# Two matrix products without a reader, placed among the first units of a retention-plus-MLP kernel

## The chip, the cores and the metric

The kernel runs on one core of one Trainium2 chip. Its time is device time in microseconds (us) of one launch on that core. TensorE is called PE in the profile, VectorE DVE, ScalarE ACT, GpSimd POOL and SyncE SP.

## What is computed

The reference has two stages. The first is a recurrent retention layer with 4 batches, 8 heads, 768 positions and head size 64:

```python
gamma = 1.0 - 2.0 ** (-5.0 - np.arange(H, dtype=np.float32))
scale = 1.0 / np.sqrt(D)
for t in range(S):
    state = gamma[None, :, None, None] * state + np.einsum('bhd,bhe->bhde', k[:, :, t], v[:, :, t])
    y[:, :, t] = scale * np.einsum('bhd,bhde->bhe', q[:, :, t], state)
```

Its output is laid out as x with 3072 rows (batch and position) and 512 columns (head and feature). The second stage is `h = x @ w_in; g = h * sigmoid(h); out = g @ w_out`, with w_in 512 x 2048 and w_out 2048 x 512.

## The kernel before

**Units and chunks.** The 768 positions are cut into 6 chunks of 128. A pair (chunk, batch) is a *unit*; there are 24, numbered chunk by chunk, so that units 0 to 3 are chunk 0 of the four batches. For each unit PE does three things, in functions that a hand-written order calls by short names:

- `T(n)` (`stage_t`, line 442): eight transposes of 128x128 through `ident` (L456), four of k and four of q, into two PSUM banks; ACT copies them out (L457).
- `SC(n)` (lines 767 to 771): the sums k^T v (`stage_s`, L482) and the scores (`stage_a`, L492), 16 small products each, into the tile `sc`. Each works on a 64x64 quarter of PE's array, and each is two records in the trace. `A(n)` then runs the next step of `steps_a`: DVE multiplies the scores by the decay mask into `am` (L500), ACT or DVE makes `mid` (L506 or L508), DVE the new `state` (L512). `Q(n)` scales the transposed q (L412), `K(n)` scales k (L407).
- `YA(n)` and `YB(n)` (`stage_y`, L531): the unit's outputs, 16 products with `am` and then those with `mid` and, after chunk 0, with `state`; between the two halves of the latter PE waits for a one-element POOL instruction (`fence`, L386). `X(n)` steps through `steps_y` and `split_x`: ACT copies the output out of PSUM (L572), and ACT and DVE split it into three fp32r parts `xt` (L587, L590, L593).

**The first product.** `P(n)` (`multiply`, line 680) is one block of x @ w_in for a whole chunk: 8 products of 512 columns into `ha` and 4 into `hb` (L684). `P(0)` needs the `xt` parts of units 0 to 3 and the first block of w_in, which ACT and DVE convert from 64-bit to 32-bit words and split (`W(i)`, lines 192 to 251 and 114 to 128). Then ACT copies `ha` (L694), DVE subtracts `hb` (L699) and ACT applies SiLU (L704).

**PSUM.** `turn(name)` (line 377) hands out the banks h0, h1 and h2 in rotation; the k half of `T(n)`, `ha` and `hb` take one each. `banks("q")`, `banks("s")` and `banks("y")` are fixed places for the q half of `T`, for `sc` and for `y`.

**Order.** Up to line 916 the order on all five engines is the order in which the program writes the calls (lines 802 to 915). PE keeps the written order to the end. After line 916 a planner orders the other engines, and the loop over `steps` (lines 961 to 1000) does the remaining first products with the remaining units folded between them. The last part (lines 1003 to 1054) is the second product, `o`, `oa` and `ob` (L1025), with g read back from DRAM.

**Around the change** (lines 823 to 834), `T`, `YA`, `YB` and `SC` are the calls that put work on PE:

```python
    X(1)
    T(3), K(3)
    X(1), X(1)
    YA(2), YB(2), X(2)
    SC(3), A(3), A(3), Q(3), A(3)
    X(2), W(1), W(1)
    X(2), X(2)
    YA(3), YB(3), X(3), X(3)
    W(1), W(1)
    T(4)
```

On PE this is: transposes of unit 3, outputs of unit 2, scores of unit 3, outputs of unit 3, transposes of unit 4, and then `P(0)`.

Of the kernel before, what the change touches and what calls it, by code (L numbers as in the profile page):

```python
# [33 lines left out]
def kernel(  # L34
# [28 lines left out]
    nc = tc.nc  # L63
    B, H, S, D = q.shape
    DM, DF = moe_w_in.shape
    C = 128
# [250 lines left out]
    ident = const.tile([128, 128], FP32, tag="ident", name="ident")  # L317
# [54 lines left out]
    def banks(tag, name, n=2):  # L372
        return ps_u.tile([128, n, 512], FP32, tag=tag, name=name)

    turns = [0]

    def turn(name):
        turns[0] += 1
        return ps_h.tile([128, 512], FP32, tag=f"h{turns[0] % 3}", name=name)
# [62 lines left out]
    def stage_t(n):  # L442
# [23 lines left out]
        for o in range(2):  # L466
            for i in range(2):
                evac[:] = [nc.scalar.copy(out=made[i][:, :, ts(o, D)], in_=tp[o][:, i]).ins]

    def score_tile(n):  # L470
        u = banks("s", f"sc_{n}")
        sc, sums = (u[:, :, ts(i, 4 * D)].rearrange("p o (a t) -> p o a t", a=HP)
                    for i in range(2))
        return sc, sums

    def stage_s(n, sums):

        kf, vs = kqv["k"].pop(n), kqv["v"][n]
        for a in range(HP):
            for o in range(2 if units[n][0] < NC - 1 else 1):  # L480
                for j in range(2):
                    nc.tensor.matmul(sums[ts(j, D), o, a, :], lhsT=kf[ts(o, D), 2 * a + j, :],  # L482
                                     rhs=vs[ts(o, D), 2 * a + j, :], start=True, stop=True,
                                     skip_group_check=True)

    def stage_a(n, sc):

        ktn = kt.pop(n)
        for a in range(HP):
            for o in range(2):  # L490
                for j in range(2):
                    nc.tensor.matmul(sc[ts(o, D), j, a, :], lhsT=ktn[ts(j, D), a, ts(o, D)],  # L492
                                     rhs=qt[n][ts(j, D), a, ts(o, D)], start=True, stop=True,
                                     skip_group_check=True)

    def steps_a(n, sc, sums):

        c, b = units[n]
        am[n] = one.tile([128, 2, HP, D], FP32, tag="am", name=f"am_{n}")
        mask = nc.vector.tensor_tensor(out=am[n], in0=sc, in1=decay, op=ALU.mult).ins  # L500
        masked[:] = [mask]
        yield
        mid = one.tile([128, HP, D], FP32, tag="mid", name=f"mid_{n}", bufs=2)
        steps_of[n] = state.get(b), mid
        if c == 0:
            nc.scalar.copy(out=mid, in_=sums[:, 0])  # L506
        else:
            nc.vector.tensor_tensor(out=mid, in0=state[b], in1=sums[:, 0], op=ALU.add)  # L508
        yield
        if c < NC - 1:  # L510
            state[b] = one.tile([128, HP, D], FP32, tag="state", name=f"state_{n}", bufs=B + 2)
            nc.vector.tensor_tensor(out=state[b], in0=mid, in1=sums[:, 1], op=ALU.add)  # L512
# [8 lines left out]
    def stage_y(n):  # L521

        vs, amn, qtn = kqv["v"].pop(n), am.pop(n), qt.pop(n)
        states = steps_of.pop(n)
        yp = banks("y", f"y_{n}")[:, :, : 4 * D].rearrange("p o (a t) -> p o a t", a=HP)

        started, done, new = set(), [], []

        def product(a, o, j, lhsT, rhs):
            e = j ^ (a % 2)  # L530
            i = nc.tensor.matmul(yp[ts(e, D), o, a, :], lhsT=lhsT, rhs=rhs,  # L531
                                 start=(e, o) not in started, stop=True,
                                 skip_group_check=True).ins
            started.add((e, o))
            if new:
                fence(done[-1], i)
                new.clear()
            done.append(i)

        def scores():  # L540
            for a in range(HP):
                for o in range(2):
                    for j in range(2):
                        product(a, o, j, vs[ts(o, D), 2 * a + j, :], amn[ts(o, D), j, a, :])

        def states_with(part):

            new.extend([part] * part)
            for a in range(HP):
                for o in range(2):  # L550
                    j = o ^ part
                    if states[o] is not None:
                        product(a, o, j, states[o][ts(j, D), a, :], qtn[ts(j, D), a, ts(o, D)])

        return scores, states_with, yp
# [6 lines left out]
    def steps_y(n, yp):  # L562
        c, b = units[n]
        if b == 0:
            p, tag = (wpool, "wq") if c == LATE else (xpool, "xt")
            xt[c] = p.tile([128, 3, KIN, NT], FP32R, tag=tag, name=f"xt_{c}")
        raw = None
        if c < LATE:
            if n == 0:
                raws.append(wpool.tile([128, LATE * B, KIN, C], FP32, tag="wq", name="ys"))  # L570
            raw = raws[0][:, n]
            nc.scalar.copy(out=raw.rearrange("p a (o t) -> p o a t", o=2), in_=yp)  # L572
        elif c == LATE:
            raw = hpool.tile([128, KIN, C], FP32, tag="hs", name=f"ys_{n}")
            nc.scalar.copy(out=raw.rearrange("p a (o t) -> p o a t", o=2), in_=yp)
            nc.sync.dma_start(out=y_dram[b], in_=raw)
        yield from split_x(c, b, yp, raw)
# [50 lines left out]
    def halves(m):  # L628
# [9 lines left out]
        if mid:  # L638
            sc, sums = score_tile(m - 1)
            stage_s(m - 1, sums)  # L640
            stage_a(m - 1, sc)
            if 1 < m <= 3 * B + 1 and units[m - 1][1] == 0:
                next_chunk()

            with queue(taken_out[0]) if m > 3 * B + 1 else ExitStack():
                finish_a(m - 1, sc, sums)
            scale_q(m - 1)
            if m > 3 * B + 1 and units[m - 1][1] == B - 1:

                behind_copy.append(next_chunk)  # L650
# [113 lines left out]
    def T(n):  # L764
        stage_t(n)

    def SC(n):
        sa[n] = sc, sums = score_tile(n)
        stage_s(n, sums)
        stage_a(n, sc)  # L770
        asteps[n] = steps_a(n, sc, sums)

    def A(n):
        next(asteps[n], None)

    def YA(n):
        ys[n] = stage_y(n)
        ys[n][0]()
        ys[n][1](0)

    def YB(n):
        ys[n][1](1)
        ysteps[n] = steps_y(n, ys[n][2])

    def X(n):
        next(ysteps[n], None)
# [3 lines left out]
    def W(i, times=1):  # L790
        if i not in slices:
            slices[i] = early_slice(i)
        for _ in range(times):
            next(slices[i], None)
# [5 lines left out]
    K, Q = scale_k, scale_q  # L800
# [22 lines left out]
    X(1)  # L823
    T(3), K(3)
    X(1), X(1)
    YA(2), YB(2), X(2)
    SC(3), A(3), A(3), Q(3), A(3)
    X(2), W(1), W(1)
    X(2), X(2)
    YA(3), YB(3), X(3), X(3)  # L830
# [172 lines left out]
    for c in range(NC):  # L1003
# [9 lines left out]
        for f in range(NF):  # L1013
            n = c * NF + f
# [3 lines left out]
            t = ready[n]  # L1018
            if f >= early_f:
                continue  # L1020
            for b in range(B):
                gh, glo, gm = (t[:, i, ts(b, C)] for i in range(3))
                oa, ob = acc[b]
                for o, g, i in (oa, gh, 0), (oa, glo, 1), (ob, gm, 2):
                    nc.tensor.matmul(o, lhsT=g, rhs=wo[f][:, i, :], start=f == 0 and i != 1,  # L1025
                                     stop=f == NF - 1 and i != 0)

        for b in range(B if early_f < NF else 0):
            oa, ob = acc[b]
            for o, parts in (ob, (2,)), (oa, (0, 1)):  # L1030
                for f in range(early_f, NF):
                    for i in parts:
                        nc.tensor.matmul(o, lhsT=ready[c * NF + f][:, i, ts(b, C)],  # L1033
                                         rhs=wo[f][:, i, :], start=False,
                                         stop=f == NF - 1 and i != 0)
        for b in range(B):
# [11 lines left out]
            n = 2 if b == B - 1 else 1  # L1048
# [36 lines left out]
```

## Time and profile before

| What | us |
|---|---|
| median of 3 runs | 619.29 |
| lowest and highest of them | 618.85, 619.48 |
| the profiled execution's own time | 621.07 |
| its span, first to last instruction | 619.2 |
| PE busy in it | 602.0 |
| DVE busy | 424.0 |
| ACT busy | 315.2 |
| DMA, mean rate | 176 GB/s |

The profile lists, for every group of instructions, its line, engine, operation and tile, its start, its length and what ended the idle time before it. Matmul ends are modelled and overlap, so the pace of PE is read from starts rather than from lengths. "PEclk" is the share of its full clock that PE was granted; the trace keeps it as a list of stretches, each with one share. "Issue" names idle time in which the engine waited for no semaphore that the profile shows.

### The profile page before, as it was taken

The page shows a single profiled execution, that of the slowest core. Times are in us where ns is not written, and L with a number is a line of the kernel's source. Part 1 is how long each engine was busy: PE and PEld are TensorE (multiplying, and loading weights), DVE is VectorE, ACT ScalarE, POOL GpSimd, SP SyncE. Part 2 cuts the span into 40 slices and gives each one's busy share as a digit, 9 for nine tenths or more (in the row PEclk, how much of TensorE's full clock was granted, in tenths as well). Part 3 has the DMA queues.
Part 4 walks back from the last instruction along what each step waited for, and adds up shares of the span by engine and source line. Part 5 has one row for each costly group of instructions (what it writes and reads, how often), then busy time and mean ns, then how long its engine had stood idle before and what let it go on. Part 6 is the DMA issues. An engine that isn't in the chain of part 4 may idle for free.

```text
span 619.2 us, 13515 instructions
## 1 busy us (share of the span) xinstructions
PE 602.0 (97%) x5384; PEld 494.0 (80%) x5384; DVE 424.0 (68%) x731; ACT 315.2 (51%) x601; POOL 29.4 (5%) x85
## 2 busy tenths in 40 slices
PE   5899999999999999999999999999999999999997
PEld 4787787888778888888788888888888888888886
DVE  4789899889988877786699783645635453654631
ACT  7568897667667656655588742312221221412311
POOL 3000000100031111120000000000000000000000
PEclk9799999999999999999999999999999999999999
DMA  9997874685699599989977542532524333442301
GB/s 191 224 227 183 224 223 154 197 242 179 218 235 231 182 252 246 291 228 270 304 228 261 190 150 68 166 106 90 184 68 131 141 103 102 139 133 89 116 1 68
DMA packets 144334, 108.88 MB, mean 176 GB/s; under 512 B 101136, under 2 KB 109584, under 8 KB 144272
## 3 DMA queue, kind: packets, MB, share of 16 engines
q1 hardware_dynamic: 141392, 102.79, 59.4%
q10 hardware_dynamic: 2880, 5.24, 2.3%
q8 instruction: 42, 0.69, 0.5%
q14 instruction: 20, 0.16, 0.1%
HBM read 66.06 MB, written 36.70 MB: 166 GB/s over the span
## 4 chain that ended last, share of the span: by engine, by line
PE 73%; DVE 5%; DMA 2%; issue 2%; ACT 2%; DVEq 0%; POOLq 0%; ACTq 0%
PE o L1025 21%; PE ha L684 18%; PE oa L1025 14%; PE hb L684 9%; PE ob L1025 7%; PE y L531 2%; DMA gd<-g 2%; DVE g L699 1%; DVE ca L219 1%; PE sc L492 1%; PE sc L482 1%; DMA wf<-in_moe_w_in_dram 0%; DVE ca L216 0%; DVE cs L224 0%; PE o L1033 0%
## 5 line engine op out<-in xcount | busy, mean ns | idle before, releaser
L684 PE MATMUL ha<-xt,wi 128*128 128x512 f32 x768 | 195.4, 396 | 1.4 <-DVE g L699 0.6
L684 PEld LDWEIGHTS ha<-xt,wi 128*128 128x128 f32 x768 | 142.9, 189 | 34.2 <-ACT wi L126 1.4
L1025 PE MATMUL o<-wo,gs 128*128 128x512 f32 x564 | 143.2, 389 | 0.0
L751 DVE TENSOR_TENSOR gs<-gr,gs 128x512 fp32r<-128x512 f32 x96 | 62.2, 686 | 90.3 <-ACT gs L749 90.3
L1025 PEld LDWEIGHTS o<-wo,gs 128*128 128x128 f32 x564 | 105.9, 188 | 21.9
L749 ACT ACTIVATE gs<-gr 128x512 fp32r<-128x512 f32 x96 | 53.6, 621 | 134.2 <-issue 131.9
L1025 PE MATMUL oa<-wo,gs 128*128 128x512 f32 x376 | 115.8, 389 | 0.0
L684 PE MATMUL hb<-xt,wi 128*128 128x512 f32 x384 | 103.0, 390 | 0.2
L699 DVE TENSOR_TENSOR g<-g,hb 128x512 f32<-128x512 f32 x96 | 65.7, 684 | 40.0 <-ACT g L694 30.2
L684 PEld LDWEIGHTS hb<-xt,wi 128*128 128x128 f32 x384 | 71.9, 188 | 16.3 <-ACT g L694 1.0
L704 ACT ACTIVATE g<-g 128x512 f32<-128x512 f32 x96 | 60.4, 629 | 46.1 <-DVE g L699 46.1
L1025 PEld LDWEIGHTS oa<-wo,gs 128*128 128x128 f32 x376 | 70.6, 188 | 14.8
L1025 PE MATMUL ob<-wo,gs 128*128 128x512 f32 x188 | 73.7, 392 | 0.0
L694 ACT ACTIVATE g<-ha 128x512 f32<-128x512 f32 x96 | 56.8, 592 | 29.4 <-PE ha L684 13.9
L752 DVE SCALAR_TENSOR_TENSOR gs<-gs 128x512 fp32r<-128x512 f32 x96 | 62.1, 684 | 0.0
L1025 PEld LDWEIGHTS ob<-wo,gs 128*128 128x128 f32 x188 | 35.3, 188 | 8.7 <-DVE o L1043 1.6
L203 ACT ACTIVATE ca<-wf 128x512 f32<-128x512 f32 x32 | 21.4, 668 | 9.5 <-DVE cw L224 5.0
L219 DVE SCALAR_TENSOR_TENSOR ca<-wf,ca 128x512 f32<-128x512 uint32 x32 | 22.7, 710 | 0.5
L1042 ACT ACTIVATE o<-o 128x512 f32<-128x512 f32 x10 | 6.0, 600 | 33.4 <-PE o L1025 33.0
L213 DVE SCALAR_TENSOR_TENSOR cs<-ca,cs 128x512 uint32<-128x512 uint32 x32 | 22.1, 691 | 0.9
L500 DVE TENSOR_TENSOR am<-sc,decay 128x512 f32<-128x512 f32 x24 | 16.5, 686 | 8.6 <-PE sc L492 8.6
L531 PE MATMUL y<-qt,mid 64*64 64x64 f32 x384 | 20.3, 224 | 0.9 <-POOL token L386 0.9
(105 smaller groups left out, 572.1 us busy)
## 6 DMA issues: line engine op xcount, KB each, us to landing
gd<-g SPq DMA_DIRECT2D x96, 256.0 KB, 3.6
gr<-gd SPq DMA_DIRECT2D x96, 256.0 KB, 2.7
wf<-in_moe_w_out_dram SPq DMA_DIRECT2D x16, 512.0 KB, 4.3
out_dram<-o ACTq DMA_DIRECT2D x20, 256.0 KB, 2.1
wf<-in_moe_w_in_dram SPq DMA_DIRECT2D x16, 256.0 KB, 4.1
wf<-in_moe_w_in_dram SPq DMA_DIRECT2D x32, 128.0 KB, 4.3
kf<-in_k_dram SPq DMA_DIRECT2D x16, 256.0 KB, 4.1
qf<-in_q_dram SPq DMA_DIRECT2D x16, 256.0 KB, 4.1
```

What stands on the lines that cost most here:

```text
L203: nc.scalar.activation(out=a.bitcast(FP32), in_=hi.bitcast(FP32), func=AF.Abs, scale=65536.0)
L213: nc.vector.scalar_tensor_tensor(out=s, in0=a, scalar=3, in1=s, op0=ALU.logical_shift_left, op1=ALU.bitwise_or)
L219: nc.vector.scalar_tensor_tensor(out=p.bitcast(FP32), in0=lo, scalar=2.0 ** -52, in1=p.bitcast(FP32), op0=ALU.mult, op1=ALU.mult)
L531: i = nc.tensor.matmul(yp[ts(e, D), o, a, :], lhsT=lhsT, rhs=rhs, start=(e, o) not in started, stop=True, skip_group_check=True).ins
L684: nc.tensor.matmul(hb if i == 2 else ha, lhsT=w_sb[f][:, i, ts(kk, 128)], rhs=xt[c][:, i, kk, :], start=kk == 0 and i != 1, stop=kk == KIN ...
L694: copied[:] = [nc.scalar.activation(out=hs, in_=ha, func=AF.Copy, scale=ONE_E).ins]
L699: taken_out[:] = [nc.vector.tensor_tensor(out=hs, in0=hs, in1=hb, op=ALU.subtract).ins]
L704: nc.scalar.activation(out=hs, in_=hs, func=AF.Silu)
L749: nc.scalar.activation(out=t[:, 0, :], in_=g, func=AF.Copy, scale=HALF)
L751: nc.vector.tensor_tensor(out=t[:, 1, :], in0=g, in1=high, op=ALU.subtract)
L752: nc.vector.scalar_tensor_tensor(out=t[:, 2, :], in0=t[:, 1, :].bitcast(FP32), scalar=-1.0 / EPS, in1=high, op0=ALU.mult, op1=ALU.add)
L1025: nc.tensor.matmul(o, lhsT=g, rhs=wo[f][:, i, :], start=f == 0 and i != 1, stop=f == NF - 1 and i != 0)
```

## The change

A helper takes the next `turn` bank and writes one product into it: the 128x128 identity as weights against the identity three times side by side (384 columns), in fp32. Nothing reads the result. It is called twice, with n = 3: between the transposes of unit 3 and the outputs of unit 2, and between the scores and the outputs of unit 3.

```diff
+
+    def keep_busy(n):
+
+        t = turn(f"none_{turns[0]}")[:, : n * C].rearrange("p (r c) -> p r c", r=n)
+        nc.tensor.matmul(t, lhsT=ident, rhs=ident.unsqueeze(1).to_broadcast([128, n, 128]),
+                         start=True, stop=True)
 
     def score_tile(n):
@@
     X(1)
     T(3), K(3)
     X(1), X(1)
+    keep_busy(3)
     YA(2), YB(2), X(2)
-    SC(3), A(3), A(3), Q(3), A(3)
+    SC(3), keep_busy(3), A(3), A(3), Q(3), A(3)
     X(2), W(1), W(1)
     X(2), X(2)
     YA(3), YB(3), X(3), X(3)
```

Each call takes one turn of the rotation, so that every later user of h0, h1 and h2 stands two places further on.

## Prediction

> **What bounds the kernel now.** I began with the page's shares and slices.
>
> ```profile
> PE 602.0 (97%) x5384; PEld 494.0 (80%) x5384; DVE 424.0 (68%) x731; ACT 315.2 (51%) x601; POOL 29.4 (5%) x85
> ...
> PEclk9799999999999999999999999999999999999999
> ```
>
> PE bounds the whole. From 60 to 610 us it is busy for 548.49 of 550 us, so a microsecond won or lost before 60 us arrives at the end almost unchanged. PEclk has one dent, in the second slice of 15.5 us. The trace's clock records give its edges: full clock from 8.847, half from 22.500 to 32.740, full until 619.83. The stretches 13.653 and 10.240 are four and three times 3.413 us, so the clock is set at the ends of windows of 3.413 us. The stretches view cut at those edges (length, PE busy and its records, granted clock, DMA share, GB/s):
>
> ```profile
> 12.26:15.67 3.41, 1.88 (x69) 1.00 1.00 179
> 15.67:19.09 3.42, 3.32 (x122) 1.00 1.05 232
> 19.09:22.50 3.41, 1.85 (x54) 1.00 0.84 213
> 22.50:25.91 3.41, 2.50 (x92) 0.50 0.88 189
> 25.91:29.33 3.42, 3.14 (x47) 0.50 1.14 245
> 29.33:32.74 3.41, 3.41 (x11) 0.50 1.12 239
> ```
>
> The poorest window, 19.09 to 22.50, stands right before the drop. PE's timeline shows why (start, length, work, and idle time before it):
>
> ```profile
> 19.44 0.68 PE L531 MATMUL y<-am,kqv 64*64 64x64 f32 x26
> 21.41 0.34 PE L531 MATMUL y<-am,kqv 64*64 64x64 f32 x6 [1.29 <-issue]
> ...
> 25.40 1.14 PE L531 MATMUL y<-am,kqv 64*64 64x64 f32 x32 [0.91 <-DVE am L500]
> ...
> 29.48 3.59 PE L684 MATMUL ha<-xt,wi 128*128 128x512 f32 x8
> 32.92 1.08 PE L684 MATMUL hb<-xt,wi 128*128 128x512 f32 x4
> ```
>
> Unit 2's outputs stop for 1.29 us in the middle, for no semaphore. Queue q8 (42 packets, 0.69 MB: 16 KB each) carries PE's instructions; one packet runs from 18.73 to 19.97, and PE goes on at 21.41. The last wait to look at is DVE's, since DVE sets the pace from 34 to 57 us:
>
> ```profile
> 24.56 0.69 DVE L500 TENSOR_TENSOR am<-sc,decay 128x512 f32<-128x512 f32 x1 [2.71 <-PE sc L492]
> ...
> 29.26 0.69 DVE L590 TENSOR_TENSOR xt<-ys,xt 128x512 fp32r<-128x512 f32 x1 [0.42 <-ACT xt L587]
> ...
> 31.65 0.69 DVE L219 SCALAR_TENSOR_TENSOR ca<-wf,ca 128x512 f32<-128x512 uint32 x1
> 34.10 0.69 DVE L699 TENSOR_TENSOR g<-g,hb 128x512 f32<-128x512 f32 x1 [1.76 <-PE hb L684]
> ```
>
> DVE idles 2.71 + 0.42 + 1.76 = 4.89 us inside the half-clock stretch, each time for PE work that runs at half pace. After 34.10 it is busy with 0.72, 0.31 and 0.27 us of waits up to 60 us.
>
> **What the skill says.** "TensorE: Matmul & The Clock Gate", "What's actually happening": a monitor halves or restores the array clock by how busy PE was in windows of 3413 ns, which run freely and don't start with the kernel. The trace agrees on windows and halves. The free-running phase I can't see from one profile; it becomes a rival. The same page, "PE-mode transpose", says transposes don't count as PE-busy in the same way. Here they must count for something (below). "FP8 and Floating Point Precision", "TensorE Precision Notes": a true fp32 product is four passes. The trace agrees: a 64-column product is two records, and records of one quarter of the array start 58.5 ns apart, 2 cycles a column each. "Runtime: NRT & Kernel Launch", "Instruction fetch mechanics": instructions come in blocks of 256 (16 KiB), mostly hidden. The block size fits; the 1.29 us shows one that isn't hidden.
>
> **How much activity keeps the clock.** I count records by their start in each window, price them in full-clock cycles (transpose 256, since they start 109 ns apart; small record 128 on a quarter of the array, so 32; 512-column record 512) and divide by 8192. 8.85: 48 small, 8 transposes, 0.44, kept. 12.26: 64 and 5, 0.41, kept. 19.09: 50 and 2, 2112 cycles, 0.26, dropped. 22.50: 82 small, 0.32, stays half. 25.91: 28 and 7, 0.33, stays half. 29.33: 8 wide and 1, 0.53, restored. Without transposes 8.85 (0.19, kept) and 19.09 (0.20, dropped) would contradict each other, so I count them. One mark near 0.34 fits all.
>
> **The change, part by part.** It removes nothing and moves no step. The compiled order of DVE, ACT, POOL and SP is the same as before but for numbering; PE has two more instructions, and the first `hb` gains a wait on PE's own earlier write, long done (estimate 0.05 us at most, hidden behind `ha`). Neither product waits for a semaphore. The two extra turns put `kp` of unit 4 on a bank that ACT emptied by 20.5.
>
> *Price of one.* No row shows 384 columns in fp32. By the records above: 2 records x 384 columns x 2 cycles = 1536 cycles, 0.64 us at full clock, 1.28 at half. Bounds: 0.17 us if one pass were enough (three quarters of the 227 ns between 512-column starts), 1.28 us at half clock. I take 0.64. A gain from the product itself is excluded, as nothing reads it; it can come only through the clock.
>
> *First product.* PE's transposes end by 19.35; it runs to 20.0. Unit 2's first records follow to about 20.6 and then meet the same missing instructions, which come at 21.41 either way, as their fetch was asked for earlier. So it costs nothing there, beyond its 4 instructions shifting the block edge (about 0.03 us). If that stall were shorter, DVE's wait for `sc` would show up to 0.64 us. It adds 1536 cycles to the window: (2112 + 1536)/8192 = 0.45, above the kept 0.41. The clock stays full at 22.50.
>
> *Unit 3's scores at full clock.* SC(4) at full clock takes 1.17 us from first start to last end. From 22.44 that ends at 23.6, and L500 starts at 23.68 instead of 24.56: 0.88 won.
>
> *Second product.* From about 23.45 to 24.1, between the scores and unit 3's outputs, which wait for `am` until 25.40 - 0.88 = 24.52. Hidden by 0.4 us. It lifts a window that has unit 3's scores and outputs, already about 0.4 at full clock.
>
> *Unit 3's outputs.* At half clock 25.40 to 27.93, 2.53 us; unit 0's at full clock 9.39 to 11.07, 1.68. End 24.52 + 1.68 = 26.20. The next instruction block bounds this: its packet lands at 24.56, and landing to use was 1.44 us before, so it is usable at 26.0 in the middle of these outputs. I take 26.5 for their end: 1.4 won.
>
> *Split and P(0).* From the copy out (27.98) to L590 (29.26) was 1.28: 26.55 + 1.28 = 27.83. DVE itself is free at 27.96 (L213, 0.88 earlier than 28.15, plus 0.69). So L590 at 27.96, L593 until 29.35, then L407, L216, L219 back to back until 31.0. PE does unit 4's transposes 26.5 to 27.5 and P(0)'s three groups of four (0.91 each) behind the split: 27.8, 28.75, 29.65 to 30.6. L699 starts at 31.0 instead of 34.10: 3.1 won, and DVE is now the later of the two.
>
> *After it.* From 34 on, DVE and PE feed each other back to back, so the shift goes through. What is late next: loads. Unit 4's k and q are issued at 18.74 and 20.40 and land after a median 4.9 and 4.7, by 25.1; needed 26.5. w_in's third block is issued until 28.45, landing about 32; its first use moves from 37.20 to 34.1. Covered, by little. I leave 0.2 us for such joints.
>
> Sum: 3.1 - 0.2 = 2.9. Profiled execution 621.07 - 2.9 = 618.2, span 616.3. The median of the runs lies 1.78 below the profiled time, so 619.29 - 2.9 = 616.4.
>
> **Rivals.**
> - *The windows lie elsewhere in timed runs.* Sliding the window over the trace, a count under 0.34 needs a start between about 18.4 and 20.0, some 1.6 of 3.41 us of phase; without the drop, the pause before P(0) offers a second weak spot. If the timed runs of before have no dip, both products lie in idle time and the result is 619.3. For it: the timed runs are 1.78 below the profiled one, and free-running windows. Against: three runs within 0.63 us, where a dip worth 3 us would split them if phases were random; that says all alike, not which.
> - *Half is kept.* A load or an instruction block comes to the joint first: w_in's block about 1.5 us later than estimated takes half of it, 617.8.
> - *Slower: the identity products count for little and the clock drops anyway.* It decides if the first adds less than 0.08 of its 0.19. Then the second starts at 24.5 at half clock, 1.28 us, and ends at 25.8 against 25.40: about 0.45 late, 619.75. If the instruction stall is also shorter in timed runs, the first adds up to 0.64 (and half the joints 0.3 more): 620.7, 0.2% slower. For it: most of the identity is zeros. Against: the counts above fit without regard to data.
> - *It doesn't do what it says* is out: both products stand in the compiled order.
>
> **Numbers.** Forecast 50%, own range 615.5 to 617.3 (best end: 3.8 of DVE's 4.89 us of idle time). Half kept 8%, no dip 30%, slower mechanism 12%. A measurement can tell about 0.2%, 1.2 us, from no change. Faster 0.55 (forecast and most of half kept), same 0.35, slower 0.10. Range 615.5 to 619.9: it takes in all cases but the slow tail.
>
> **What would show it.** Right: no clock record of half between 9 and 619 us; L500 near 23.7; L699 near 31.0; each product two records over some 0.64 us; the 1.29 us pause shrunk to about 0.7. Wrong: a half-clock stretch of 10.24 us elsewhere; L699 early but PE waiting for a DMA or for issue before 57 us; or a trace as predicted with timed runs that don't move, which would mean that they had no dip to lose.

## The result and the profile after

| What | before | after |
|---|---|---|
| median of 21 timed runs each, us | 619.48 | 621.87 |
| lowest and highest, us | 617.70, 622.03 | 619.44, 624.89 |
| profiled execution, own time and span, us | 621.07 and 619.2 | 623.06 and 621.2 |

The ratio of after to before is 1.0036, with a 95% interval of 1.0021 to 1.0051: 0.4% slower, where the prediction said 0.5% faster (616.4, range 615.5 to 619.9).

Executions more than 1.5% above the fastest of their kernel are left out of the ratios, and of the counts of timed runs further down.

The early part went almost as predicted. The page of after, shares and slices:

```profile
PE 601.8 (97%) x5388; PEld 491.8 (79%) x5388; DVE 424.3 (68%) x731; ACT 314.8 (51%) x601; POOL 28.8 (5%) x85
...
PEclk9999999999999999989999999999999999999999
```

The dent of the second slice is gone, and a small new one stands in the eighteenth (264 to 280 us). PE's timeline of after, from unit 3's transposes to the first product (start, length, work, idle time before it):

```profile
19.14 0.81 PE L473 MATMUL none<-ident 128*128 128x384 f32 x2
19.88 0.69 PE L537 MATMUL y<-am,kqv 64*64 64x64 f32 x32
...
22.40 0.91 PE L473 MATMUL none<-ident 128*128 128x384 f32 x2
23.39 0.69 PE L537 MATMUL y<-am,kqv 64*64 64x64 f32 x32
23.92 0.28 PE L537 MATMUL y<-qt,mid 64*64 64x64 f32 x4
25.54 0.33 PE L537 MATMUL y<-qt,mid 64*64 64x64 f32 x4 [1.34 <-issue]
...
27.98 2.12 PE L690 MATMUL ha<-xt,wi 128*128 128x512 f32 x8 [0.33 <-ACT xt L593]
29.94 1.08 PE L690 MATMUL hb<-xt,wi 128*128 128x512 f32 x4
```

All of it runs at full clock: the eight products of `ha` take two microseconds instead of three and a half. The pause for no semaphore that stood at 20.12 inside unit 2's outputs is gone, but one of 1.34 us now stands inside unit 3's outputs, 24.20 to 25.54. DVE's timeline of after shows the lead handed on:

```profile
22.55 0.69 DVE L506 TENSOR_TENSOR am<-sc,decay 128x512 f32<-128x512 f32 x1 [0.81 <-PE sc L498]
...
27.96 0.69 DVE L596 TENSOR_TENSOR xt<-ys,xt 128x512 fp32r<-128x512 f32 x1 [1.14 <-ACT xt L593]
...
31.13 0.69 DVE L705 TENSOR_TENSOR g<-g,hb 128x512 f32<-128x512 f32 x1
```

The subtraction of `hb` starts at 31.13 instead of 34.10, 2.97 us earlier. The following table sets the start of the same wide products of both kernels side by side (after minus before, from the two traces):

| near, us of before | 40 | 140 | 165 | 238 | 270 | 299 | end |
|---|---|---|---|---|---|---|---|
| after minus before, us | -2.98 | -3.4 | -3.53 | -3.01 | +0.42 | +2.0 | +1.97 |

So the lead lives for 165 us and is lost, and more than lost, between 165 and 300. What PE waits for from 165 to 345 us, first in after and then in before (total, times, longest, us):

```profile
PE hb L690 <- ACT g L700: 2.7, 1, 2.7
PE ha L690 <- DVE g L705: 0.4, 1, 0.4
PE y L537 <- POOL token L386: 0.3, 1, 0.3
PE hb L690 <- DVE xt L599: 0.2, 1, 0.2
```

```profile
PE ha L684 <- DVE g L699: 0.6, 1, 0.6
PE y L531 <- POOL token L386: 0.3, 1, 0.3
```

Before has no wait longer than 0.6 us there; after has one of 2.7 us. PE's timeline of after at that place:

```profile
265.28 1.98 PE L690 MATMUL ha<-xt,wi 128*128 128x512 f32 x8
269.95 1.20 PE L690 MATMUL hb<-xt,wi 128*128 128x512 f32 x4 [2.69 <-ACT g L700]
270.98 3.51 PE L690 MATMUL ha<-xt,wi 128*128 128x512 f32 x8
```

PE stands still for 2.69 us until ACT has copied the earlier product out, and the clock is then halved for one window, 271.10 to 274.51 (`ha` takes 3.51 us instead of 1.98), which costs 1.6 us more.

ACT came late to that copy. Followed back, its last wait (2.62 us, until 268.27) is for DVE, and DVE's is for the store of a block of converted w_out, `wod<-cw`, which must land before DVE may write the buffer `cw` anew. DVE's line in after and then in before, where it waits for nothing:

```profile
267.54 0.69 DVE L224 TENSOR_TENSOR cw<-cs,ca 128x512 f32<-128x512 f32 x1 [1.49 <-DMA wod<-cw]
```

```profile
267.11 0.69 DVE L224 TENSOR_TENSOR cw<-cs,ca 128x512 f32<-128x512 f32 x1
```

That store took 6.8 us to land in after and 3.4 us in before. So DVE is here 0.43 us later than in before, and the 2.3 us of lead that PE still had at 255 us are lost in its wait. Before that, ACT itself had waited for transfers. Its waits for them from 225 to 285 us, in after and then in before:

```profile
ACT g L700 <- DMA gd<-g: 7.4, 4, 3.3
ACT ca L203 <- DMA wf<-in_moe_w_out_dram: 3.6, 1, 3.6
```

```profile
ACT g L694 <- DMA gd<-g: 3.5, 2, 2.2
ACT ca L203 <- DMA wf<-in_moe_w_out_dram: 2.8, 1, 2.8
```

`gd<-g` is the store of g, which must land before ACT may write the buffer `hs` anew. Both kernels do the same transfers. The packets of the main queue fill 92.7% of the 16 engines' time from 165 to 300 us in before and 95.1% in after, so one may suppose that a store that comes out late has little room to catch up. But the fullness by itself doesn't tell a kernel that loses time here from one that doesn't: before run once more (`again`, below) has 97.3% and loses nothing.

### The profile page after: what moved, and what is told of

The parts are those of the page before. It is cut to its first block, busy times and chain, and to the rows that moved or that the text cites. A ratio compares the mean times of both kernels' runs of the same rounds, so it can differ in the third digit from the quotient of the medians.

```text
span 621.2 us, 13524 instructions
## 1 busy us (share of the span) xinstructions
PE 601.8 (97%) x5388; PEld 491.8 (79%) x5388; DVE 424.3 (68%) x731; ACT 314.8 (51%) x601; POOL 28.8 (5%) x85
## 4 chain that ended last, share of the span: by engine, by line
PE 67%; DMA 6%; DVE 6%; ACT 2%; issue 2%; SPq 1%; DVEq 0%; ACTq 0%; POOLq 0%
PE o L1032 21%; PE ha L690 15%; PE oa L1032 14%; PE hb L690 8%; PE ob L1032 7%; DMA gd<-g 3%; DVE g L705 1%; DMA wod<-cw 1%; DMA wf<-in_moe_w_out_dram 1%; PE y L537 1%; DMA yr<-yd 1%; DVE ca L219 1%; DVE cw L224 1%; ACT g L700 1%; DVE xt L596 1%
```

## The experiments

Five theories stand behind the expectations, by letter. **A**: an early arrival is paid for later, since loads and stores come no sooner. **B**: the added instructions cost something by themselves. **C**: the two extra turns of h0, h1 and h2 cost something. **D**: the added PE instructions move the places at which 16 KB blocks of 256 instructions cut PE's program. **E**: it is instructions at just those two places.

"Late loss" below is the length of the stretch from one wide product to a later one (164.7 to 345.0 us in before, 180.29 us long) in the experiment's trace, less 180.29. It leaves out all that happens early. Each is one traced execution; medians and ratios are of 11 to 22 timed runs, set against before's runs of the same series. In all eighteen traces DVE, ACT, POOL and SyncE do the same operations in the same order (an added memset or copy apart), so no theory of another order is needed.

### Columns, places, an early lead

`tiny` keeps both products but cuts them to one column:

```diff
-        nc.tensor.matmul(t, lhsT=ident, rhs=ident.unsqueeze(1).to_broadcast([128, n, 128]),
-                         start=True, stop=True)
+        nc.tensor.matmul(t[:, 0, :1], lhsT=ident, rhs=ident[:, :1], start=True, stop=True)
```

> Both products cut to one column: the instructions, their places and the turns of the banks stay as in the change, the activity that held the clock goes. Theory A (the clock is held and units arrive 3 us earlier at the later stage, where stores and loads pace the kernel and the lead turns into waits): the half-clock stretch near 22 us is back, L705 of the first block near 34.1, time as before, ratio 0.998 to 1.001. Theory B (the shifted banks or the four to eight extra instructions cost it): as slow as the change, ratio 1.003 to 1.005.

`first` keeps only the first product, `second` only the second:

```diff
-    SC(3), keep_busy(3), A(3), A(3), Q(3), A(3)
+    SC(3), A(3), A(3), Q(3), A(3)
```

> Only the product ahead of unit 2's outputs. It alone lifts the window of 19 to 22.5 us to 0.45 by the count of the prediction, so the clock should hold there; the pause before the first product may still drop it some 3 us later in part of the executions. Theory A: where the clock holds, L705 near 31 and the time near that of the change, ratio 1.002 to 1.005; theory B: between before and the change, about 1.002.

```diff
-    keep_busy(3)
     YA(2), YB(2), X(2)
```

> Only the product behind unit 3's scores. It comes after the poor window, so the clock should drop near 22 us as before and the product runs at half clock for 1.28 us, about 0.45 us of it in the way. Theory A: no lead, ratio 1.000 to 1.002. Theory B: about half of the loss, 1.002.

`late` is the change and, behind `P(0)`, five more such products that delay PE by about the lead:

```diff
+    t = banks("q", "none_q", 1)[:, 0, : 3 * C].rearrange("p (r c) -> p r c", r=3)
+    for _ in range(5):
+        nc.tensor.matmul(t, lhsT=ident, rhs=ident.unsqueeze(1).to_broadcast([128, 3, 128]),
+                         start=True, stop=True)
```

> The change, and five more such products (3.2 us of PE at full clock) behind the first block of the first product, ahead of unit 4's scores: the lead of 3 us is taken away there by plain work, with the clock held. Theory A (it is the early arrival that is paid for later): time back at that of before or 0.2% around it, ratio 0.999 to 1.002, though there is more work. Theory B (what is lost lies in the added instructions and banks themselves): slower than the change by the 3 us, ratio 1.007 to 1.009.

| kernel | median, us | ratio [95%] | at 165 us | late loss, us |
|---|---|---|---|---|
| after | 621.87 | 1.0036 [1.0021, 1.0051] | -3.53 | +5.55 |
| tiny | 623.88 | 1.0064 [1.0039, 1.0088] | -0.35 | +2.99 |
| first | 622.78 | 1.0027 [1.0004, 1.0051] | -2.00 | +2.11 |
| second | 622.25 | 1.0025 [1.0006, 1.0044] | -1.33 | +2.83 |
| late | 625.09 | 1.0070 [1.0047, 1.0093] | -0.19 | +2.48 |

`tiny` and `late` reach 165 us with no lead worth the name and still lose 3.0 and 2.5 us afterwards: A falls as the common cause, though in after's trace 2.3 us of lead are lost in one wait. The columns seem to help: `tiny` has the same instructions as after and none of the activity, and its ratio is the higher of the two (of different series, with intervals that overlap).

### Nothing at all, and the rotation

`again` is before once more, unchanged; `turns` takes the two turns without a product; `yq` writes the products into the y and q banks instead, and `tiny_yq` is that with one column.

> The kernel before once more, as a control of the comparison itself and for a second trace of it. Every theory: ratio 1.000, within 0.15%. If it comes out 0.2% slower, a difference of that size between two kernels says nothing. Its trace shows how far one execution differs from another in the stage from 170 to 300 us.

```diff
+    turn("none_a")
     YA(2), YB(2), X(2)
-    SC(3), A(3), A(3), Q(3), A(3)
+    SC(3), turn("none_b"), A(3), A(3), Q(3), A(3)
```

> The kernel before with two turns of the banks taken at the places of the products, and no product: the banks of every later block are rotated as in the change, no instruction is added. Theory C (the rotated banks cost it): 1.002 to 1.004. Theory D (the added PE instructions move the edges of the 256-instruction blocks, so that PE runs out of instructions at worse places): 1.000.

```diff
-        t = turn(f"none_{turns[0]}")[:, : n * C].rearrange("p (r c) -> p r c", r=n)
+        t = banks(tag, f"none_{tag}", 1 if tag == "q" else 2)[:, 0, : n * C].rearrange("p (r c) -> p r c", r=n)
```

> The two products with their 384 columns written into the banks of unit 2's outputs and of unit 4's q, which are free then, so that the rotation of the other banks stays as before. Theory C: faster than before, as the clock is held and nothing is rotated, 0.996 to 0.998. Theory D: as slow as the change, 1.002 to 1.005.

> The same with one column each: no rotation, no activity, only the added instructions. Theory C: as before, 1.000. Theory D: 1.003 to 1.007, as the one-column products had with the rotation.

| kernel | median, us | ratio [95%] | at 165 us | late loss, us |
|---|---|---|---|---|
| again | 620.91 | 1.0001 [0.9980, 1.0022] | -0.22 | -0.13 |
| turns | 620.04 | 0.9994 [0.9972, 1.0017] | -2.30 | -0.10 |
| yq | 621.81 | 1.0035 [1.0005, 1.0065] | -2.94 | +1.42 |
| tiny_yq | 623.71 | 1.0055 [1.0038, 1.0072] | +0.13 | +2.49 |

`turns` arrives 2.3 us early at 165 and keeps it to the end: against A once more. C isn't needed for the loss: the median and the trace of `turns` show none, and `yq`, which takes no turn, is as slow as after. A second trace of before loses nothing.

### PE instructions elsewhere

`pad2`, `pad6` and `pad16` are before with 2, 6 and 16 products of 1x1 at the very start of PE (8, 24 and 64 instructions), `after_pad61` is after with 61 of them: 244 instructions, with the change's own nearly one whole block.

```diff
+    pad = const.tile([1, 1], FP32, tag="pad", name="pad")
+    nc.vector.memset(pad, 0.0)
+    none = banks("y", "none_y")[:1, 0, :1]
+    for _ in range(2):
+        nc.tensor.matmul(none, lhsT=pad, rhs=pad, start=True, stop=True)
     T(0), K(0)
```

> The kernel before with two 1x1 products (8 PE instructions) in PE's idle time ahead of everything, and none at the places of the change: it takes no time of its own, but every later edge of a 256-instruction block falls 8 instructions earlier in the program, as in the change. Theory D (the edges' places cost the time): 1.003 to 1.006, as the one-column products. Theory E (what costs is an instruction at those two places, for the waits or the clock there): 1.000.

> Six such products at the start, edges 24 instructions earlier. Theory D: another ratio than that of two, anywhere from 0.997 to 1.007, as other steps of the program are cut. Theory E: 1.000.

> Sixteen such products at the start, edges 64 instructions earlier. Theory D: again another ratio, 0.997 to 1.007. Theory E: 1.000.

> The change with 61 such products at the start: 244 instructions, with the change's own 9 nearly a whole block, so that the edges cut the program within 3 to 5 instructions of where they cut it before; at the start they may delay the first transposes by up to 2 us. Theory D: faster than the change by 0.3 to 0.6%, ratio to before 0.996 to 1.001. Theory E: no faster than the change, 1.003 to 1.007.

Then, to tell the place of the cuts from the number of instructions, exactly one block (`pad64`), half a block (`pad32`) and one product (`pad1`); only the count in the diff above changes.

> The kernel before with 64 products of 1x1 at the very start of PE: 256 PE instructions, one whole fetch block, so that later blocks cut the program where they cut it in before. D (the cut places): the stretch from 165 to 345 us keeps before's length within 0.3 us, although the whole program is one block further on and starts about 2 us later; median 621 to 624 by the late start alone. Rival (any added PE instruction costs, wherever the cuts fall): that stretch is 1.5 to 3 us longer, as with 8, 24 and 64 added instructions.

> 32 such products, 128 PE instructions, half a block. D: the cuts lie as far from those of before as they can, so the stretch from 165 to 345 us is 1.5 to 3 us longer; median 622 to 624. Rival (the cost grows or falls with the number of instructions and not with the cuts): between the values of 64 and of 256 added instructions.

> One such product, 4 PE instructions. D in its sharp form (a cut moved by two products already costs): stretch from 165 to 345 us 1 to 3 us longer, median about 622. D in its soft form (only cuts moved by more than a few products cost): the stretch within 0.3 us of before's, median 619.5 to 620.5.

| kernel | PE instructions added | median, us | ratio [95%] | at 165 us | late loss, us |
|---|---|---|---|---|---|
| pad1 | 4 | 621.78 | 1.0030 [1.0009, 1.0052] | -1.31 | +0.56 |
| pad2 | 8 | 622.74 | 1.0048 [1.0028, 1.0068] | +0.29 | +3.51 |
| pad6 | 24 | 622.46 | 1.0041 [1.0021, 1.0060] | -0.92 | +2.08 |
| pad16 | 64 | 622.91 | 1.0042 [1.0020, 1.0065] | -1.88 | +1.79 |
| pad32 | 128 | 622.12 | 1.0041 [1.0020, 1.0062] | -3.76 | +2.24 |
| pad64 | 256 | 622.23 | 1.0030 [1.0011, 1.0049] | +2.95 | +0.07 |
| after_pad61 | 244 + 9 | 623.74 | 1.0070 [1.0045, 1.0095] | +4.37 | +0.13 |

E falls: eight instructions that do nothing, at the start of the program, cost as much as the change. The late losses are as D says: 0.6 us for 4 instructions, 1.8 to 3.5 us for 8 to 128, and 0.1 us for 253 and 256, although the whole program is then one block further on.

The medians are less clear. `pad64` and `after_pad61` are slow too, and lose their time early: by unit 0's first sums they are 1.6 and 1.5 us late, by 80 us 3.2 and 4.9, with half-clock windows in between (from 30.71 and 58.02 in `pad64`, from 60.35 in `after_pad61`) and pauses at cuts. For `pad64` the 1.6 us of the start are most of what its median is slower by, 0.30%. `after_pad61` missed D's expectation, 0.996 to 1.001: its median is 0.70% slower, and 0.46% when 1.5 us are taken off for the start, no better than after. There is a rival, too: both reach 165 us three to four us later than before, which no other kernel does, and a late arrival may spare them the late transfers. No run separates that from the place of the cuts.

Two traces show the cut itself. In the late stage of `pad32`, PE's timeline:

```profile
186.41 0.64 PE L492 MATMUL sc<-qt,kt 64*64 64x64 f32 x31
189.09 0.27 PE L492 MATMUL sc<-qt,kt 64*64 64x64 f32 x1 [2.04 <-issue]
```

The last of 32 score records waits 2.04 us for no semaphore. Counting PE's records from the start and from zero, weight loads and the sequencer's records among them, the pause stands at number 5313, which is 193 + 20 x 256. This is no accident of one trace: the eighteen traces have 47 pauses of PE of over 0.2 us for no semaphore, and every one stands at 193 or 194 + 256k, with k a whole number. This is what places the cuts. The 16 KB packet ahead of it ran from 186.63 to 187.67. This one pause is most of the 2.24 us lost. In `pad16` the same view has one pause of 1.12 us, of a late loss of 1.79:

```profile
197.92 0.21 PE L531 MATMUL y<-qt,mid 64*64 64x64 f32 x1 [1.12 <-issue]
```

PE's waits of `pad64` from 165 to 345 us are those of before, to the tenth:

```profile
PE ha L684 <- DVE g L699: 0.6, 1, 0.6
PE y L531 <- POOL token L386: 0.3, 1, 0.3
```

### A clock without so many instructions

`lean` has two one-pass products in bf16 of 512 columns at the first place alone, into the y bank: 4 instructions and no turn.

```diff
+    idb = const.tile([128, 128], mybir.dt.bfloat16, tag="idb", name="idb")
+    nc.vector.tensor_copy(out=idb, in_=ident)
...
+        t = banks("y", "none")[:, 0, : n * C].rearrange("p (r c) -> p r c", r=n)
+        one_pass = idb.unsqueeze(1).to_broadcast([128, n, 128])
+        for _ in range(2):
+            nc.tensor.matmul(t, lhsT=idb, rhs=one_pass, start=True, stop=True)
...
+    keep_busy(4)
     YA(2), YB(2), X(2)
```

> The first place of the change alone, with two products in bf16 of 512 columns into the y bank in place of one in fp32 of 384: 4 PE instructions in place of 8 or 9, no turn of the rotation, and 1024 full-array cycles, which lift the poor window from 0.26 to 0.38 of it. D, soft: the clock is kept and the late stretch is not longer; median 617 to 619, faster than before. D, sharp: the clock is kept and the late stretch is 1 to 3 us longer; median 620 to 622. If 0.38 is too little for the clock, the dip stays as often as in before: 619.5 to 622.

Measured: 621.52, ratio 1.0024 [1.0006, 1.0041], late loss +3.35 us, with a wait of PE for ACT of 1.9 us near 270 us as in after. So the gain was not to be had this way. It also limits D: `lean` and `pad1` shift the late cuts by the same 4 instructions, and one lost 3.35 us, the other 0.56, which is between D's two forms. A shifted cut makes the loss possible; its size depends on something more, or differs from one execution to the next, since the medians of the two are alike (621.52 and 621.78). No version here beats before.

### What the timed runs say of the clock

Each timed run comes with its mean granted clock; one window of 3.41 us at half clock lowers it by 0.003. Of before's 253 timed runs in the four series of experiments, 89 have no dip to speak of (clock at least 0.9985, mean time 618.9), 91 about one window of half clock (at least 0.9955, 620.4), and 73 a larger dip (622.3). So the dip of the profiled execution, three windows, was there in a minority of the runs. Runs with the larger dip:

| kernels | larger dip |
|---|---|
| before | 73 of 253 |
| `again` (before once more) | 10 of 21 |
| after, yq (384 columns) | 3 of 21, 3 of 14 |
| tiny, tiny_yq (same places, 1 column) | 12 of 17, 11 of 18 |
| pad2, pad6 (no product there) | 12 of 22, 10 of 21 |

The columns do what they are for, 6 of 35 against 23 of 35 with the same instructions. Whether the instructions by themselves make dips more frequent is less sure: `again` adds none, and its 10 of 21 are as many as those of `pad2` and `pad6`.

Runs without a dip are slower than before's as well: the 10 of after have a mean of 620.8 us, 1.9 above the 618.9 of before's (1.2 above the series of before with the slowest such runs, 619.57). But the 7 of `turns` have 620.1, 1.6 above its own series' 618.5, and its trace has no late loss. So these runs don't show by themselves that it is the late loss that costs the time, and a cost of the rotated banks, made up for by fewer dips (2 of 14), can't be excluded.

## Why the prediction was wrong

- **The clock at the first product: right.** The prediction had the full clock kept, the scores' mask at 23.68 (measured 22.55), `P(0)` from 27.8 to 30.6 (27.98 to about 31.0), and the subtraction at 31.0 (31.13). Its 3.1 us came out as 2.97. The price of one product, 0.64 us, came out as 0.74 (19.14 to 19.88). In part this is luck: the mask came 1.1 us earlier than said, because no pause for instructions was ahead of it, and the pause of 1.34 us inside unit 3's outputs took that time back. The first split of unit 3 on DVE, at 27.96 in both, was to wait for DVE's own work, and waited 1.14 us for ACT.
- **"So it costs nothing there, beyond its 4 instructions shifting the block edge (about 0.03 us)": the step that failed.** The term of 0.03 us priced the shift as the time in which PE consumes four instructions. In the runs the added instructions cost far more than that: where they come without columns (`tiny`, `tiny_yq`, `pad2`, `pad6`, `pad16`, `pad32`) the median rises by 0.41 to 0.64%, 2.5 to 4.0 us. In the traces of these six kernels 1.8 to 3.5 us are lost between 165 and 345 us, and 0.1 where a whole block is added. What matters, as far as these traces go, is where each of the later cuts falls. The prediction leaned on the Trainium skill, "Runtime: NRT & Kernel Launch", section "Instruction fetch mechanics", which has the sequencer fetch the next block while the current one runs and calls the crossing mostly hidden. It reckoned with two cuts that aren't hidden, both in the first 30 us, and with none of the later ones. The runs disagree with the page where PE runs small products: pauses of 1.34 (after), 1.12 (`pad16`) and 2.04 us (`pad32`) stand at the cuts.
- **"From 34 on, DVE and PE feed each other back to back, so the shift goes through": failed too.** It does go through to 165 us (-3.53 there). In after's trace 3.9 us are then lost up to and with the wait of 2.69 us, and 1.6 us in the stretch with the window of half clock behind it, 5.55 together. The leftover of 0.2 us "for such joints" looked at joints before 57 us; the ones that opened were after 165 us, at stores for which DVE and ACT wait. That the moved cuts opened them in after isn't shown.
- **The sum was made for one execution and carried to the median: nearly twice too large.** The rival "the windows lie elsewhere in timed runs" had 30% and was half right. A larger dip was in 29% of before's runs, about one window in 36%. The argument against it, three runs within 0.63 us, was chance: before's 253 runs spread from 616.7 to 626.0. Even without any dip the mean of before, 620.4 over those runs, would fall only to 618.9: some 1.5 us to win, not 2.9.
- **The slower rival had another mechanism** (products that count for little, 619.75 to 620.7). It falls, since full-width products cut the larger dips from 23 of 35 to 6 of 35. The slowdown came by a way that no rival named.
- **In the medians:** the instructions without columns cost 4.0 us (`tiny`, 0.64% of 620.88), and the columns give back about 1.7 (0.64% less 0.36%, which sets ratios of two series against each other; between `tiny_yq` and `yq`, of one series, it is 1.2, and the intervals overlap in both pairs). That leaves the 0.36% measured, 2.2 us.

**What stays open.** That added instructions cost this much is shown. That they do so by the place of the cuts is supported, by the whole-block traces without a late loss and by two traces with the pause at the cut itself, but not settled: the medians don't set the whole-block kernels apart, and their late arrival is an untested rival. Even in the first 60 us equal places don't pause alike: `pad64` and `after_pad61` pause 1.50 and 1.16 us at a cut (number 1217) at which before, `again` and `turns` (number 961) don't pause.

In the other kernels with shifted cuts, after among them, PE waits for ACT (1.0 to 2.7 us in seven of eleven), ACT and DVE for stores and loads; the wait of DVE for `wod<-cw` near 267 us, 1.49 us in after, is there in six of the ten others (0.4 to 1.1 us) and in none of the five traces without a loss. How a moved instruction packet makes those transfers late isn't shown, but they are late: w_out's blocks, issued from 165 to 300 us, land after a median of 4.8 to 5.2 us in the five traces without a loss and of 5.4 to 6.0 in the thirteen others, apart from `pad1` (5.0, which lost 0.56) and `pad16` (4.7, where the pause is most of the loss). One store shows both things side by side, the first of four stores of g issued in a row (at 201.60 in before, at 198.28 in after). In the five traces without a loss a packet of PE's instructions starts 1.4 to 2.4 us ahead of it, and it lands after 4.7 to 5.2 us. In the nine with 4 to 9 instructions added the packet starts 2.7 to 3.0 us ahead, and it lands after 6.0 to 7.1 us. That the one causes the other would still have to be tested. The late loss is from one trace of each kernel, so how often it occurs in the timed runs isn't known.

## What to carry to other kernels

Instructions put into an engine's idle time can cost more than the time in which they run; here a few that did nothing cost 2.5 to 4.0 us. They move every later place at which instruction blocks are cut, and where small products use up a block faster than the next one comes, a cut can become a pause. Test such an edit against a version with as many idle instructions that do nothing, and one with exactly one block of them. And before a clock dip is priced from a profile, look at how many of the timed runs have it.

## What was not expected of the hardware

- A cut can be dear where PE's instructions are short. In the first 60 us of after, the packet for the next block comes late: PE passed the cut at record 705 at 20.2, the packet for the one after it ran from 22.75 to 24.00, and PE went on with record 961 at 25.54. That is 5.3 us from cut to cut for 256 records that PE had worked off in 4.0 (20.2 to 24.20).
- The pause at a cut differs from execution to execution of one kernel: at the cut inside unit 2's outputs it was 1.29 us in before's trace and 0.70 in that of `again`, and at 55 us 0.23 and 1.75. So a single trace doesn't tell what a moved cut will cost. In after the first of these is gone and one of 1.34 us stands a block later, but `pad2`, with no product there, pauses at both places (0.74 and 1.34 us).
- In after's trace one idle stretch of 2.69 us, late in a stage in which PE is otherwise always busy, was followed by a whole window of half clock (271.10 to 274.51). That stall was paid for twice, 2.7 and 1.6 us. `lean` had a wait of 1.88 us at nearly the same place and kept its clock.
